# Two attentions on one core: copies of Q and K tied to their rounded parts, halo reads placed with Q, another order for the last output groups and for the first unit's value parts

## Chip, core and metric

The kernel runs on one core of one Trainium2 chip. The metric is the device time of one execution in microseconds (us). The core has five engines that the text names: TensorE (PE in the profile; PEld is its weight load), VectorE (DVE), ScalarE (ACT), GpSimd (POOL) and SyncE (SP). SyncE does no arithmetic here; it issues the DMAs that copy Q and K, and a DMA that waits on its queue holds up those behind it.

## What is computed

Two attention layers over separate inputs, each with S = 2048 positions, D = 1024 and 32 heads of 32. B attends to a sliding window of 256 positions; A attends to 8 positions at a distance of 2.

```python
def _A_ref(x, wqkv, wo):
    H = 32; Dh = D // H
    W, dil = 8, 2
    qkv = (lambda x, *d: x.transpose(*d))((x @ wqkv).reshape(B, S, 3, H, Dh), 2, 0, 3, 1, 4)
    q, k, v = qkv[0], qkv[1], qkv[2]
    ...
    logits = jnp.einsum("bhsd,bhswd->bhsw", q, kg) * scale
    logits = jnp.where(mask[None, None, :, :], logits, -1e9)
    attn = _softmax(logits, axis=-1)
    o = jnp.einsum("bhsw,bhswd->bhsd", attn, vg)
    return (lambda x, *d: x.transpose(*d))(o, 0, 2, 1, 3).reshape(B, S, D) @ wo

def _B_ref(x, wqkv, wo):
    H = 32; Dh = D // H; W = 256
    ...
    scores = jnp.einsum("bhqd,bhkd->bhqk", q, k) * (Dh ** -0.5)
    idx = jnp.arange(S)
    mask = (idx[:, None] - idx[None, :] >= 0) & (idx[:, None] - idx[None, :] < W)
    scores = jnp.where(mask[None, None], scores, -1e9)
    p = _softmax(scores, axis=-1)
    o = jnp.einsum("bhqk,bhkd->bhqd", p, v)
    return (lambda x, *d: x.transpose(*d))(o, 0, 2, 1, 3).reshape(B, S, D) @ wo
...
return jnp.concatenate([a, b], axis=-1)
```

## The kernel before

**Units, slots, head groups.** Each layer's 2048 positions are cut into four chunks of 512, so there are eight units: 0 to 3 are layer B (called dense: 256 positions back), 4 to 7 are layer A (called windowed; its even and odd positions are sorted apart, so that distance 2 becomes distance 1). A unit that continues the one before it has a halo: units 1, 2, 3, 5 and 7 read the last K columns of the unit before. In each unit the 32 heads are taken in eight slots of four heads. Unit u, slot s is head group 8u + s; there are 64.

**Two parts of every number.** Every operand of a projection is held as a rounded part and a low part (the difference to the rounded one), and a product is three matmuls (`TERMS`, L30). `Stream` (L87) loads each weight or input tile of 128 x 1024 into one of three raw buffers, by GpSimd's DMA queue after the first eight, and `parts` (L126) splits it: VectorE casts (L129), and VectorE (L137) or GpSimd (L134) subtracts. Weights go whole into one of three w tiles; inputs are split in halves into ten x tiles.

**The work of a slot.** `qk_items` (L298) multiplies for Q, then K: 24 wide matmuls each (L363). `evac` (L311) lets ScalarE write the rounded part out of PSUM (L314) and VectorE the low part (L318). Then `stack` (L323) issues three copies (L328) by SyncE into a stacked tile, `qst` or `kst`, of 96 rows: rounded, rounded, low for Q and rounded, low, rounded for K, so that one score matmul over 96 rows sums the three products. There are two `qst` and two `kst`, used in turn; `waiting` holds a stack back until the head group two before has given out its result. For units with a halo, `read_halo` (L304) issues three more reads into `kst`, and L333 writes the halo of the next unit. `attention` (L589) then makes a first pass of 16 scores (L614) whose row maximum (L619, VectorE) and exponential sum (L624, ScalarE) give the log sums; these go through a small transpose (L653) and by SyncE (L660) as two more rows into `qst`. A second pass (L696 dense, L509 windowed) has the logarithm of the sum already in it; ScalarE takes the exponential, masks follow on VectorE or GpSimd, and the matmuls with V (L741, L548) give the result `ot`, again in two parts (L577, L581). `v_items` (L395) makes the values of a unit in four parts, in the slots of `V_SLOTS`; `o_items` (L438) multiplies a finished unit by wo, in the slots of `O_SLOTS` of the next unit, eight groups of 24 wide matmuls (L455). A group's result is copied to the single staging tile `ost` (`NST` is 1; L379 ScalarE or L382 VectorE) and stored by ScalarE's queue (L470). For the last unit, `TAIL` groups run seven of their eight steps (a step is one head group's `ot`) before the last head group has its result, and the eighth step after it; the other groups follow whole.

**The order.** `tc.manual_schedule()` is on: every engine runs its instructions in the order in which the Python program emits them. That order comes from a planner, the loop at L803: it holds a clock of its own (`Clock`, L33) with a price for every operation, takes from four sequences (log sums, second passes, first passes, projections) the item that could start first, and emits it. `done["stack"]` tells when the planner believes K's copies to have landed, `done["nat"]` when a Q or K is copied out. The chip does not see this clock: there each instruction waits on semaphores for its operands.

## Time and profile before

| | |
|---|---|
| time, median of 3 runs | 1974.42 us (1971.13 to 1975.38) |
| time of the profiled execution | 1973.82 us |
| its span, first to last instruction | 1972.1 us |
| mean granted clock of TensorE | 0.987 |
| busy: TensorE, VectorE, ScalarE, GpSimd | 98%, 66%, 49%, 36% |

A share is of the span. A row of the timeline gives the start, how long the row's instructions take together, the engine, the line, what is written and read, and in brackets the idle time of the engine before it with what ended it. A row of the chain gives start, length and what was on the chain that ended last. A row of stretches gives the bounds, the length, the busy time of PE, PEld, DVE, ACT and POOL with their counts of instructions, the granted clock of TensorE, the share of the DMA engines and the GB/s. A row of waits names who waited for whom: us in total, times, longest.

### The profile page before, as it was taken

To read this page: it belongs to the slowest core of one execution; us is meant where nothing else is said; L and a number is where in the kernel's file an instruction comes from. 1 tells how busy PE (TensorE), PEld (TensorE's weight loads), DVE (VectorE), ACT (ScalarE), POOL (GpSimd) and SP (SyncE) were. 2 spreads that over 40 slices of the span, in tenths; PEclk is the share of its full clock that TensorE was granted. 3 is DMA by queue.
4 is the path that set the end of the run, shared out by engine and by line. 5 is a ranking of instruction groups with operands and counts; after the bars stand their busy time and mean duration, and the time that the engine had idled before them with its cause. 6 is when DMAs were issued, how large, how long until landed. Compare 5 with 4: busy or idle time off the path is not lost.

```text
span 1972.1 us, 36479 instructions
## 1 busy us (share of the span) xinstructions
PE 1924.7 (98%) x12608; PEld 1619.8 (82%) x12608; DVE 1295.7 (66%) x3762; ACT 957.5 (49%) x3137; POOL 708.7 (36%) x923
## 2 busy tenths in 40 slices
PE   7999999999999999999999999999999999999998
PEld 6878887888877878788878888978888788888886
DVE  5687776678665786567865657655666557666653
ACT  3565554475654656555563344423534334434441
POOL 4334343444433434443443323233332333233221
PEclk9999999999999999999999999999989999999998
DMA  5555546455546465345645647455553565556442
GB/s 176 150 139 153 160 124 178 132 153 157 152 136 174 121 189 149 117 140 148 177 119 146 173 139 196 128 149 170 149 163 116 174 177 162 141 146 172 136 126 75
DMA packets 136502, 294.92 MB, mean 150 GB/s; under 512 B 14464, under 2 KB 42112, under 8 KB 136320
## 3 DMA queue, kind: packets, MB, share of 16 engines
q1 hardware_dynamic: 85632, 124.82, 26.1%
q0 software_dynamic: 40320, 146.82, 22.9%
q10 hardware_dynamic: 10368, 20.98, 2.9%
q8 instruction: 100, 1.64, 0.4%
q14 instruction: 82, 0.67, 0.1%
HBM read 163.58 MB, written 27.26 MB: 97 GB/s over the span
## 4 chain that ended last, share of the span: by engine, by line
PE 84%; DVE 7%; DMA 6%; ACT 2%; issue 1%; SPq 0%; POOL 0%; DVEq 0%; ACTq 0%; POOLq 0%
PE g L363 31%; PE g L455 16%; PE g L415 16%; PE s L614 7%; PE s L696 5%; PE o L741 4%; PE s L509 3%; DMA qst<-rt 3%; PE o L548 2%; DMA kst<-nat 1%; DMA raw<-xs 1%; DVE x L137 1%; DVE w L129 1%; ACT s L624 1%; DVE w L137 1%
## 5 line engine op out<-in xcount | busy, mean ns | idle before, releaser
L363 PE MATMUL g<-x,w 128*128 128x512 f32 x3072 | 801.9, 401 | 8.6 <-DVE w L129 8.0
L134 POOL TENSOR_TENSOR w<-raw,w 128x512 fp32r<-128x512 f32 x225 | 392.5, 1745 | 897.2 <-PE s L614 285.7
L363 PEld LDWEIGHTS g<-x,w 128*128 128x128 f32 x3072 | 562.0, 191 | 110.9 <-DVE w L129 8.4
L624 ACT ACTIVATE s<-s,nm 128x384 f32<-128x384 f32 (+3 forms) x1024 | 452.3, 443 | 231.0 <-DVE nm L619 227.1
L415 PE MATMUL g<-w,x 128*128 128x256 f32 x3072 | 413.3, 285 | 0.0
L415 PEld LDWEIGHTS g<-w,x 128*128 128x128 f32 x3072 | 392.7, 191 | 1.9 <-issue 0.6
L455 PE MATMUL g<-ot,w 128*128 128x512 f32 x1536 | 384.2, 397 | 3.6 <-DVE w L129 2.9
L455 PEld LDWEIGHTS g<-ot,w 128*128 128x128 f32 x1536 | 283.8, 190 | 58.1 <-DVE w L129 3.6
L619 DVE CUSTOM_DVE_ANT_0 s<-s,mask_d 128x384 f32<-128x384 f32 (+2 forms) x512 | 262.0, 556 | 72.9 <-PE s L614 71.5
L614 PE MATMUL s<-kst,qst 96*128 96x384 f32 (+3 forms) x1024 | 238.7, 303 | 16.2 <-ACT s L624 7.1
L701 ACT ACTIVATE pbuf<-s 128x384 f32<-128x384 f32 (+2 forms) x480 | 197.1, 507 | 85.5 <-PE s L696 81.8
L614 PEld LDWEIGHTS s<-kst,qst 96*128 96x128 f32 x1024 | 181.3, 192 | 60.5 <-ACT s L624 18.1
L624 ACT ACTIVATION_READ_ACCUMULATOR s<-s,nm 128x1 f32 x1024 | 210.2, 205 | 0.0
L619 DVE CUSTOM_DVE_ANT_0 s<-s,mask_w 128x136 f32<-128x136 f32 (+1 forms) x512 | 142.4, 322 | 98.4 <-PE s L614 96.8
L129 DVE CAST w<-raw 128x1024 fp32r<-128x1024 f32 x256 | 199.9, 781 | 9.4 <-PE g L455 9.4
L137 DVE TENSOR_TENSOR w<-raw,w 128x512 fp32r<-128x512 f32 x287 | 197.2, 696 | 8.8
L682 POOL TENSOR_SCALAR_AFFINE_SELECT pbuf<-pbuf 128x128 f32<-128x128 f32 (+1 forms) x383 | 147.9, 404 | 150.1 <-ACT pbuf L701 143.5
L314 ACT ACTIVATE nat<-g 128x512 fp32r<-128x512 f32 x128 | 76.6, 598 | 255.2 <-PE g L363 247.8
L318 DVE SCALAR_TENSOR_TENSOR nat<-g,nat 128x512 fp32r<-128x512 f32 x128 | 88.3, 690 | 145.5 <-ACT nat L314 134.9
L524 DVE TENSOR_TENSOR pbuf<-pbuf,keep_w 128x272 f32<-128x272 f32 (+1 forms) x224 | 116.9, 566 | 61.5 <-ACT pbuf L514 60.6
L619 DVE DVE_READ_ACCUMULATOR2_ANT nm<- 128x1 f32 x1024 | 144.3, 141 | 0.0
L696 PEld LDWEIGHTS s<-qst,kst 98*128 98x128 f32 x704 | 106.2, 189 | 37.8 <-PE o L741 10.0
(48 smaller groups left out, 1227.3 us busy)
## 6 DMA issues: line engine op xcount, KB each, us to landing
raw<-wqk POOLq DMA_DIRECT2D x126, 512.0 KB, 3.7
qst<-nat SPq DMA_DIRECT2D x192, 256.0 KB
kst<-nat SPq DMA_DIRECT2D x192, 256.0 KB
raw<-wo POOLq DMA_DIRECT2D x64, 512.0 KB, 3.7
raw<-wv POOLq DMA_DIRECT2D x62, 512.0 KB, 4.5
outs<-ost ACTq DMA_DIRECT2D x64, 256.0 KB
raw<-xs POOLq DMA_DIRECT2D x28, 512.0 KB, 4.8
halo<-nat SPq DMA_DIRECT2D x40, 256.0 KB
```

Source lines behind the costliest of these rows:

```text
L129: nc.vector.tensor_copy(t[:, 0, :], raw)
L134: nc.gpsimd.tensor_tensor(o, a, b, op=ALU.subtract)
L137: nc.vector.tensor_tensor(o, a, b, op=ALU.subtract)
L363: nc.tensor.matmul(h["ps"], h["w"][:, a, k * P:(k + 1) * P], xt[u][k][:, b, :], start=(k == 0 and i == 0), stop=(k == NK - 1 and i == 2))
L415: nc.tensor.matmul(ps, xt[u][k][:, a, p0:p0 + P], h["w"][:, c, k % kw], start=(k == 0 and i == 0 and r == 0), stop=(k == NK - 1 and i == 2 ...
L455: nc.tensor.matmul(h["ps"], h["w"][:, a, k * P:(k + 1) * P], ot[u, k][:, b, :], start=(k == 0 and i == 0), stop=(k == NK - 1 and i == 2))
L614: nc.tensor.matmul(ps[:, :n], q[0:96, j, b * P:(b + 1) * P], kk[0:96, j, c0:c1], start=True, stop=True)
L619: nc.vector.tensor_tensor_reduce(ps[:, :n], ps[:, :n], mask[:, cut:full], scale=-1.0, scalar=BIG, op0=ALU.add, op1=ALU.min, accum_out=nm)
L624: nc.scalar.activation(ps[:, :n], ps[:, :n], AF.Exp, bias=nm, scale=-1.0, accum_out=sm)
L682: nc.gpsimd.affine_select(w, w, pattern=[[0, m], [step, n]], compare_op=ALU.is_ge, fill=0.0, base=base, channel_multiplier=chan)
L696: nc.tensor.matmul(ps[:, i * n:(i + 1) * n], kk[0:98, j, 256 + kb * P:256 + (kb + 1) * P], q[0:98, j, q0:q0 + n], start=True, stop=True)
L701: nc.scalar.activation(w, ps[:, :pack * n].rearrange("p (j n) -> p j n", j=pack), AF.Exp)
```

## The change

The copies out of the rounded part are put into the program when the rounded part is begun (`stack_hi`), the copy out of the low part when that is made (`stack`); both use `place`. The halo reads stand ahead of Q's copies, and no longer ahead of K's. The last unit's output groups have `TAIL` 4: four groups run seven eighths early; group 3 accumulates in a bank of the score ring `rs`, and the weights of groups 3 to 7 (kind "xw") are split in halves into x tiles. In the first unit the value parts stand in slots 0, 2, 4, 7. Two prices of the planner change: a load by GpSimd's queue and VectorE's score pass. Line numbers of the diff are those of the source before and after.

```diff
@@ -24,8 +24,9 @@
 VPARTS = ((0,2),(2,2),(4,2),(6,2))
 V_SLOTS = {0: 0, 1: 1, 5: 2, 7: 3}
 O_SLOTS = {2: (0, 1), 3: (2, 3), 4: (4, 5), 5: (6, 7)}
+V0_SLOTS = {0:0,2:1,4:2,7:3}
 NX, NST = 10, 1
-TAIL, LAND, XAT = 2, 0.45, 1
+TAIL, LAND, XAT = 4, 0.45, 1
 C1, C3, CG, CV = 0.114, 0.2, 0.231, 0.243
 TERMS = ((0, 0), (0, 1), (1, 0))
 
@@ -60,7 +61,7 @@
 
     def fetch(self, dur, *ready):
 
-        t = max(self.use("pool", 1.0, *ready) + 0.6, self.free["loads"])
+        t = max(self.use("pool", 0.6, *ready) + 0.9, self.free["loads"])
         self.free["loads"] = t + dur + 0.5 * max(0.0, min(2 * dur, self.free["copies"] - t))
         return self.free["loads"] + LAND
 
@@ -109,7 +110,7 @@
             i = self.split
             self.load_to(i + 1)
             raw, t0 = self.raw.pop(i)
-            if self.items[i][0] == "x":
+            if self.items[i][0] != "w":
                 self.tiles[i], self.ready[i] = [], []
                 for h in range(2):
                     t = self.xpool.tile([P, 2, S], F32R, tag="x", name="x")
@@ -120,7 +121,7 @@
                 self.ready[i] = self.parts(t, raw, t0)
                 self.tiles[i] = t
             self.split += 1
-            end = self.ready[i] if self.items[i][0] != "x" else max(self.ready[i])
+            end = self.ready[i] if self.items[i][0] == "w" else max(self.ready[i])
             self.ck.defer(end, lambda n=i + NRAW + 1: self.load_to(n))
 
     def parts(self, t, raw, t0):
@@ -173,8 +174,9 @@
             if u and s in O_SLOTS:
                 plan += [("o", u - 1, n) for n in O_SLOTS[s]]
             plan.append(("qk", u, s))
-            if s in V_SLOTS:
-                plan.append(("v", u, V_SLOTS[s]))
+            vs = V_SLOTS if u else V0_SLOTS
+            if s in vs:
+                plan.append(("v", u, vs[s]))
         if u + 1 < U:
             plan.append(("x", u + 1))
     plan += [("o", U - 1, n) for n in range(NG)]
@@ -195,7 +197,7 @@
     for p in plan:
         ly = units[p[1]][0]
         if p[0] == "o":
-            item(p, "w", wo[ly, p[2]])
+            item(p, "w" if p[1] < U - 1 or p[2] < 3 else "xw", wo[ly, p[2]])
         elif p[0] == "v":
             s0, n = VPARTS[p[2]]
             for g in range(n):
@@ -321,24 +323,37 @@
                 rg.give(bank, e)
 
                 def stack():
-                    if t == 1 and has_halo:
-                        read_halo()
-                    dst, c = (qst[buf], 0) if t == 0 else (kst[buf], 256)
-                    for i, a in enumerate((0, 0, 1) if t == 0 else (0, 1, 0)):
-                        nc.sync.dma_start(dst[i:96:3, :, c:c + S].bitcast(F32), hl[:, a, :].bitcast(F32))
-                        e2 = ck.copy(0.95, e, ck.now)
+                    e2 = place(1, e)
                     if t == 1:
-                        done["stack"][u, s] = e2
+                        done["stack"][u, s] = max(e2, h2["hi"])
                     if t == 1 and u + 1 < U and units[u + 1][3]:
                         nc.sync.dma_start(halo[u % 2][s], hl[:, :, 256:].bitcast(F32))
                         e2 = ck.copy(0.95, e, ck.now)
-                    done["nat"][hg, t] = e2
-
+                    done["nat"][hg, t] = max(e2, h2["hi"])
+
+                later(stack)
+
+            def place(part, e):
+                dst, c = (qst[buf], 0) if t == 0 else (kst[buf], 256)
+                for i, a in enumerate((0, 0, 1) if t == 0 else (0, 1, 0)):
+                    if a == part:
+                        nc.sync.dma_start(dst[i:96:3, :, c:c + S].bitcast(F32), hl[:, a, :].bitcast(F32))
+                        e2 = ck.copy(0.95, e, ck.now)
+                return e2
+
+            def stack_hi():
+                if t == 0 and has_halo:
+                    read_halo()
+                h2["hi"] = place(0, r)
+
+            def later(f):
                 if hg < 2 or hg - 2 in done["o"]:
-                    stack()
+                    f()
                 else:
-                    waiting.setdefault(hg - 2, []).append(stack)
-
+                    waiting.setdefault(hg - 2, []).append(f)
+
+            h2 = {}
+            later(stack_hi)
             ck.defer(r, low)
 
         for t in range(2):
@@ -438,24 +453,32 @@
     def o_items(u, n):
         h = {}
 
+        last = u == U - 1
+        ring = rs if last and n == 3 else rg
+
         def ready(k):
             if (u * NG + k) not in done["ot"]:
                 return None
             if k == 0:
                 st.split_to(where["o", u, n] + 1)
-                h["r"] = st.ready[where["o", u, n]]
-                return latest(rg.when(), h["r"], done["ot"][u * NG])
-            return done["ot"][u * NG + k]
+                r = st.ready[where["o", u, n]]
+                h["r"] = r if isinstance(r, list) else [r, r]
+                return latest(ring.when(), h["r"][0], done["ot"][u * NG])
+            return max(done["ot"][u * NG + k], h["r"][k // 4])
 
         def run(k):
             if k == 0:
-                h["ps"], h["b"] = rg.take()
-                h["w"], _ = st.get(where["o", u, n])
+                h["ps"], h["b"] = ring.take()
+                w, _ = st.get(where["o", u, n])
+                h["w"] = [(w[i // 4], i % 4 * P) if isinstance(w, list) else (w, i * P) for i in range(NK)]
+            w, c = h["w"][k]
             for i, (a, b) in enumerate(TERMS):
-                nc.tensor.matmul(h["ps"], h["w"][:, a, k * P:(k + 1) * P], ot[u, k][:, b, :],
+                nc.tensor.matmul(h["ps"], w[:, a, c:c + P], ot[u, k][:, b, :],
                                  start=(k == 0 and i == 0), stop=(k == NK - 1 and i == 2))
-            if k == 3 and (u < U - 1 or n != TAIL - 1):
-                st.split_to(where["o", u, n] + 2)
+            if k == 3 and (not last or n == 0 or n > 2):
+                st.split_to(where["o", u, n] + (3 if last and n == 0 else 2))
+            if k == 5 and last and n in (1, 2):
+                st.split_to(where["o", u, n] + 3)
 
         def after(k):
             if k == NK - 1:
@@ -463,7 +486,7 @@
                 for f in list(stores.values()):
                     f()
                 o = stp.tile([P, S], F32, tag="ost", name="ost")
-                e = copy_out(o, h["ps"], h["b"], rg)
+                e = copy_out(o, h["ps"], h["b"], ring)
 
                 def store():
                     if stores.pop((u, n), None):
@@ -618,7 +641,7 @@
             def top():
                 nc.vector.tensor_tensor_reduce(ps[:, :n], ps[:, :n], mask[:, cut:full], scale=-1.0, scalar=BIG,
                                                op0=ALU.add, op1=ALU.min, accum_out=nm)
-                e = ck.use("dve", (n + 80) / 960, ck.now)
+                e = ck.use("dve", (n + 110) / 960, ck.now)
 
                 def total():
                     nc.scalar.activation(ps[:, :n], ps[:, :n], AF.Exp, bias=nm, scale=-1.0, accum_out=sm)
```

## The prediction

> **What bounds the kernel now.** I read the page first: span, busy shares, clock, chain of waits.
>
> ```profile
> span 1972.1 us, 36479 instructions
> PE 1924.7 (98%) x12608; PEld 1619.8 (82%) x12608; DVE 1295.7 (66%) x3762; ACT 957.5 (49%) x3137; POOL 708.7 (36%) x923
> PE 84%; DVE 7%; DMA 6%; ACT 2%; issue 1%; SPq 0%; POOL 0%; DVEq 0%; ACTq 0%; POOLq 0%
> ```
>
> TensorE is busy for 98% of the span and carries 84% of the chain; the next engine has a third of its time free. The change adds no matmul and takes none away (both programs hold the same number of each kind), so it can only move time through the 47.4 us in which TensorE is idle (1972.1 - 1924.7) and through the clock at which it runs. I therefore listed next what ends the waits of TensorE, over the whole span.
>
> ```profile
> PE s L614 <- ACT s L624: 7.1, 8, 1.2
> PE s L509 <- DMA qst<-rt: 6.7, 10, 1.8
> PE s L614 <- DMA kst<-nat: 5.7, 5, 2.0
> ```
>
> Columns: us in total, times, longest. Score matmuls (L614) wait for the copy of K into its stacked tile five times, 5.7 us in all, once for 2.0. The last reading is of stretches: busy time of each engine, then the granted clock.
>
> ```profile
> 1542.40:1545.80 3.40, 2.06 (x10) 1.36 (x8) 0.00 (x0) 0.59 (x1) 0.58 (x1) 1.00 1.07 328
> 1545.80:1549.20 3.40, 3.14 (x18) 2.79 (x19) 2.05 (x12) 1.97 (x10) 0.00 (x0) 1.00 0.58 223
> 1453.70:1463.90 10.20, 10.20 (x36) 8.95 (x36) 5.84 (x19) 4.83 (x16) 1.92 (x2) 0.50 0.41 115
> 1917.90:1921.30 3.40, 2.04 (x13) 1.51 (x12) 0.14 (x1) 0.10 (x1) 0.00 (x0) 1.00 0.02 5
> 1921.30:1938.40 17.10, 13.54 (x73) 9.99 (x73) 10.39 (x17) 4.24 (x10) 3.11 (x4) 0.50 0.18 61
> ```
>
> In 1453.70 to 1463.90 and in 1921.30 to 1938.40 the granted clock is 0.50: a wait on TensorE can cost more than itself. The latter follows a stretch in which TensorE had 2.04 us of work in 3.40. The first two rows show that it is not certain: as little work at 1542.40, and the clock stayed at 1.00 behind it. At half clock 17.1 us give 8.5 us of work less.
>
> **The copies of Q and K.** Stated aim: the copies of the rounded part leave while the low part is made. Here is one K of the kernel before (unit 6, slot 2, windowed), from its last matmul to the first score matmul.
>
> ```profile
> 1536.81 1.52 PE L363 MATMUL g<-x,w 128*128 128x512 f32 x6
> 1538.17 6.28 PE L455 MATMUL g<-ot,w 128*128 128x512 f32 x27
> 1538.37 0.60 ACT L314 ACTIVATE nat<-g 128x512 fp32r<-128x512 f32 x1 [4.84 <-PE g L363]
> 1539.00 1.93 SPq L328 DMA_DIRECT2D kst<-nat  x3
> 1539.01 0.69 DVE L318 SCALAR_TENSOR_TENSOR nat<-g,nat 128x512 fp32r<-128x512 f32 x1 [3.42 <-ACT nat L314]
> 1546.06 0.63 PE L614 MATMUL s<-kst,qst 96*128 96x128 f32 x4 [1.60 <-DMA kst<-nat]
> ```
>
> ScalarE ends the rounded part at 1538.97; the first copy is issued at 1539.00, before VectorE has begun the low part at 1539.01. The queue waits for data, not for the place in the source text, and the source already put a rounded copy first. VectorE is done at 1539.70, and the three issues last until 1540.93 at 0.64 each, so the low copy is ready before its turn. The edit only swaps the second and third copy of K; for Q it swaps nothing. On the chip it is worth 0.
>
> What does move is the planner's own clock. It dates the copies from the rounded part (time r) instead of the low part (time e), and its constants then put the end of K's three copies 5.32 us behind K's last matmul, where they gave 6.09 (0.82 to r, 0.77 more to e, 1.20 to issue, 3 x 0.95 to move, 0.45 to land; now the third copy waits only for the two before it, and the 0.77 falls out). The order of TensorE is written out from that clock, so the first score matmuls are set earlier. I counted the matmuls between K's last and the first score of each of the 64 head groups, in both programs, at the pace of the rows: 0.23 us for 512 columns, 0.125 for 256, 0.11 to 0.18 for the small ones.
>
> ```profile
> 44.23 5.49 PE g L363 x24
> 148.17 3.79 PE g L415 x30
> ```
>
> The cover's median falls from 8.2 to 6.3 us, its minimum from 6.1 to 5.5, and groups with under 6.6 us go from 7 to 36. An example: in unit 5, slot 2, 36 wide matmuls (8.2 us) stood between; now 27 (6.2).
>
> What is needed? In the fence above 7.73 us (1538.33 to 1546.06), of which the last copy takes 5.65 from its issue. The opposite bound is unit 4, slot 2, where the score starts without a wait 6.11 us behind K's end (1078.86 to 1084.97):
>
> ```profile
> 1540.32 5.65 DMA kst<-nat
> 1073.71 5.15 PE L363 MATMUL g<-x,w 128*128 128x512 f32 x22
> 1084.97 0.64 PE L614 MATMUL s<-kst,qst 96*128 96x128 f32 x4
> ```
>
> Summing the shortfall over all 64 groups, by what one copy is taken to need: 6.1 us gives 0 before and 5.6 after; 6.6 gives 1.6 and 21.8; 7.0 gives 5.8 and 36.2. The trace's own 5.7 us, spread over few long waits, says that the typical need is below 7.0; 7.73 for all is excluded, since it would give 17 before. I take 6.6, between the bounds: **22 us after, 16 more than now**; ends 0 and +30. TensorE runs in order, so the projection matmuls that could fill such a wait stand queued behind the score; VectorE, ScalarE and the next loads are late with it, and nothing of the wait lies beside other work.
>
> Some of these waits will halve the clock, as the first unit's did (the longest K wait, 2.0 us, then 3.4 us at 0.50):
>
> ```profile
> 30.30:33.70 3.40, 1.39 (x12) 1.22 (x11) 0.19 (x1) 0.00 (x0) 0.00 (x0) 1.00 0.93 297
> 33.70:37.10 3.40, 3.40 (x18) 3.40 (x18) 3.13 (x15) 2.31 (x11) 1.75 (x2) 0.50 0.04 14
> ```
>
> With needs from 6.1 to 7.7 on covers near 5.9, some six of 36 would exceed 1.3 us. If half of them cost one stretch of 3.4 us at 0.50 (1.7 us), that is 5, less 1.7 that this first wait has already: **+3**, ends 0 and +12.
>
> **Halo reads.** They go with Q instead of K. Before, in unit 5, slot 2:
>
> ```profile
> 1301.87 1.86 SPq L328 DMA_DIRECT2D qst<-nat  x3
> 1303.78 2.05 SPq L308 DMA_DIRECT2D kst<-halo  x3
> 1306.69 0.60 ACT L314 ACTIVATE nat<-g 128x512 fp32r<-128x512 f32 x1 [4.84 <-PE g L363]
> 1307.31 1.95 SPq L328 DMA_DIRECT2D kst<-nat  x3
> ```
>
> The reads left 2.9 us before K's rounded part was even begun; K's copies are not behind them. Ahead of Q they can add at most their 2.05 us of issue to Q, whose score stands 11.3 us or more behind Q's last matmul in the new order: 0 either way. The row of log sums (qst<-rt) is never put behind a waiting halo read in the new queue order; once, in unit 0, it stands behind two Q copies.
>
> **The end.** Four output groups instead of two run seven eighths before the last window, group 3 in a score bank, and the weights of groups 3 to 7 are split in halves into x tiles (for VectorE two short casts in place of a long one, and both subtractions, while TensorE has 5.5 us of work a group). Before:
>
> ```profile
> 1917.51 0.22 PE L653 MATMUL s<-ident,hl 128*32 128x128 f32 x1
> 1918.07 0.67 SPq L660 DMA_DIRECT2D qst<-rt  x1
> 1920.52 3.80 PE L509 MATMUL s<-qst,kst 98*128 98x8 f32 x20 [1.36 <-DMA qst<-rt]
> 1926.45 0.59 ACT L577 CAST ot<-o 128x512 fp32r<-128x512 f32 x1 [1.50 <-PE o L548]
> 1927.09 3.23 PE L455 MATMUL g<-ot,w 128*128 128x512 f32 x6 [0.70 <-ACT ot L577]
> 1929.08 0.59 ACT L379 COPY ost<-g 128x512 f32<-128x512 f32 x1 [2.04 <-PE g L455]
> 1931.83 0.69 DVE L382 COPY ost<-g 128x512 f32<-128x512 f32 x1 [4.06 <-DMA outs<-ost]
> 1932.43 0.69 DVE L129 CAST w<-raw 128x1024 fp32r<-128x1024 f32 x1
> 1933.17 1.22 PE L455 MATMUL g<-ot,w 128*128 128x512 f32 x2 [2.85 <-DVE w L129]
> ```
>
> Three waits (1.36 + 0.70 + 2.85 = 4.9) and 8.5 of half clock: 13.4 us. In the new order 15 wide matmuls (3.45) stand between L653 and the first window matmul, which needs 2.8: no wait. Twelve plus the 24 of group 3 (at least 5 us) lie between the last window matmuls and the first that needs the last ot: no wait. But there is still one output staging tile. The copies of groups 1, 2 and 3 all stand on VectorE, each behind the landing of the store before it (copy ended 1929.67, next began 1931.83: 2.16, plus 0.60 for itself), and the split of group 5 stands behind them. From the start of the last eighths: ScalarE's copy ends at 1.45, the three copies begin at 3.6, 6.4 and 9.1, the cast at 9.7, the matmul at 10.2. TensorE has 4 x 0.69 + 5.5 = 8.3 us to do. So a wait of 1.9, and behind it likely 1.7 to 3.4 of half clock: some 4.4 instead of 13.4, **-9**; ends -12 (no wait, no half clock) and -3.
>
> **First unit, prices.** The value parts of unit 0 move from slots 1, 5, 7 to 2, 4, 7; its TensorE waits other than K's are under 1 us each. The prices (VectorE's score pass, POOL's loads) move 54 instructions from VectorE to POOL and elsewhere; both have the time (66% and 36%). Where a unit ends, in units 4 to 6, the row of log sums gets 5.5 us of cover instead of 3.3 to 4.7; in units 1 and 2, slot 6, it gets 2.1, under the 3.14 that this copy takes here:
>
> ```profile
> 1185.43 3.14 DMA qst<-rt
> ```
>
> Together **-1**, ends -8 and +6.
>
> **Sum** on the profiled execution (1973.8 us, 0.6 under the median shown): +16 + 3 - 9 - 1 = +9: 1982.8, and against the median **1983**.
>
> **A rule against the trace.** The row at 1917.90 had 1.36 us of idle in a 3.40 us stretch and was followed by half clock. The Trainium skill, "TensorE: Matmul & The Clock Gate", "What's actually happening", says that the clock falls back only after a whole idle window of about 3.4 us; by that no wait here would cost clock, and the trace disagrees (0.50 after 1.36 us of idle).
>
> **Rivals.**
> - Slower still: K needs 6.9 or more as a rule, and every second wait over 1 us halves the clock. +27 + 12 - 8 = 2005. For it: 7.73 above. Against: only five such waits before.
> - Faster: the scores' wait on K. If K's copies, with nothing beside them, need about 6.1, the waits stay at 5.7, the end gives 9 and the unit ends 3: 1962. It decides at a need of about 6.3, where the waits after reach 12 and the sum is 0. For it: the row at 1084.97. Against: the wait at 1546.06 behind 6.28 us of work.
> - No change: a wait on K makes up for a later wait on loads or log sums (7.1 and 6.7 us are there to be absorbed), so that 9 of the 16 vanish: 1974.
> - Waits cost only themselves: no half clock follows waits of under 3 us, at K or at the end. 1983 - 3 - 2.5 = 1978 (2.5 is the end's half clock). Against it: the two rows at 0.50. The rule of the Trainium skill above would give this case.
>
> **How the numbers follow.** Chances: forecast 0.48 (its own range 1977 to 1993), slower still 0.16, faster 0.20, no change 0.10, waits alone 0.06. About 0.2% is what a measurement of this kernel can tell: under 1970.5 is faster, over 1978.4 slower. The last case lies at the edge, and I count half of it as slower: faster 0.20, same 0.13, slower 0.67. The range takes half of each outer rival: 1963 to 2000.
>
> **What would show it.** Right: TensorE waits for kst<-nat some 25 to 36 times, near 22 us in all; K's first copy still issued within 0.1 us of ScalarE's end, the last at 2.0; one wait of about 2 us at group 5 of the end, and the span from the last log-sum row to the end shorter. Wrong: kst<-nat waits under 10 us, or K's copies landing sooner after K's last matmul than now, or a gain at unit ends over 8 us.

## The result, and the profile after

| | before | after |
|---|---|---|
| median of the runs compared | 1974.3 us | 2000.5 us (1991.8 to 2001.4) |
| ratio, 95% interval | | 1.0134 [1.0105, 1.0162] |
| time of the profiled execution | 1973.8 us | 1991.8 us |
| its span | 1972.1 us | 1990.0 us |

The kernel became 26 us slower; forecast were 9, with a range up to 2000. The profiled execution of after is its fastest; its granted clock is 0.994, that of the other three 0.990 to 0.991, so the traces show 18 of the 26 us. The page of after:

```profile
span 1990.0 us, 36510 instructions
PE 1924.5 (97%) x12608; PEld 1611.6 (81%) x12608; DVE 1277.4 (64%) x3708; ACT 955.2 (48%) x3130; POOL 744.8 (37%) x989
PE 80%; DMA 8%; DVE 6%; issue 2%; ACT 2%; POOL 1%; SPq 0%; DVEq 0%; ACTq 0%; POOLq 0%
```

TensorE is idle for 65.5 us (1990.0 - 1924.5) where it was for 47.4: 18.1 more, about the whole difference of the spans. Two further changes cancel. The clock was better (lost to it: 0.006 x 1990 = 12 us, before 0.013 x 1972 = 26). And TensorE's work at full clock, which is its busy time less what the clock took, grew by 13.5 us, from 1899.1 to 1912.6, for the same matmuls. Counted from start to start of the matmuls outside the half-clock stretches, 6 us of that lie in value matmuls of 384 columns; the rest is spread in pieces under 3.5 us. The profile models where a matmul ends, so a stall between two matmuls can stand in the busy time; what stalls here stays open. What ends the idle time, in the view of waits (us in total, times, longest):

```profile
PE s L637 <- DMA kst<-nat: 14.8, 15, 3.1
PE s L719 <- DMA qst<-rt: 6.9, 6, 1.7
PE s L637 <- issue: 5.5, 8, 2.3
PE s L532 <- DMA qst<-rt: 4.2, 8, 1.1
PE s L637 <- DMA kst<-halo: 2.9, 4, 1.0
PE g L476 <- DVE x L130: 2.1, 1, 2.1
```

L637 is the first pass of scores (L614 before). Its wait for K grew from 5.7 to 14.8 us, and some waits for K stand under other names: those put down to "issue" and to the halo read end at the same matmul. So below I count by place instead: the idle time straight before the first score matmul of each of the 64 head groups. That is **6.1 us (8 times) before, 24.4 (32 times) after**. The place that the prediction took as its example (unit 6, slot 2) in the timeline of after:

```profile
1560.68 0.84 PE L378 MATMUL g<-x,w 128*128 128x512 f32 x3
1561.36 6.28 PE L476 MATMUL g<-ot,w 128*128 128x512 f32 x27
1561.56 0.60 ACT L316 ACTIVATE nat<-g 128x512 fp32r<-128x512 f32 x1 [4.84 <-PE g L378]
1562.18 1.85 SPq L340 DMA_DIRECT2D kst<-nat  x3
1562.19 0.69 DVE L320 SCALAR_TENSOR_TENSOR nat<-g,nat 128x512 fp32r<-128x512 f32 x1 [3.42 <-ACT nat L316]
1569.98 0.63 PE L637 MATMUL s<-kst,qst 96*128 96x128 f32 x4 [2.35 <-issue]
```

The first copy leaves 0.02 us after ScalarE's end (1562.16), as before. At this place the same 27 matmuls of 6.28 us stand ahead of the score in both kernels. The score starts 8.46 us behind K's last matmul (1561.52), against 7.73 before: here the score was not put earlier, K came later, and the wait is 2.35 instead of 1.60. Over all 64 head groups the order did what the prediction counted: TensorE's work between K's last matmul and the first score has a median of 6.4 us, before 8.0, and 36 groups have less than 6.6, before 7.

The end of after, from the timeline, and then its stretches (busy time of the five engines, then the granted clock):

```profile
1932.22 0.92 PE L430 MATMUL g<-w,x 128*128 128x256 f32 x6
...
1942.37 0.22 PE L676 MATMUL s<-ident,hl 128*32 128x128 f32 x1 [0.57 <-DVE hl L668]
...
1960.02 0.59 ACT L394 COPY ost<-g 128x512 f32<-128x512 f32 x1 [5.77 <-PE g L476]
...
1962.78 0.69 DVE L397 COPY ost<-g 128x512 f32<-128x512 f32 x1 [7.81 <-DMA outs<-ost]
1965.64 0.69 DVE L397 COPY ost<-g 128x512 f32<-128x512 f32 x1 [2.17 <-DMA outs<-ost]
1968.51 0.69 DVE L397 COPY ost<-s 128x512 f32<-128x512 f32 x1 [2.18 <-DMA outs<-ost]
1969.12 0.42 DVE L130 CAST x<-raw 128x512 fp32r<-128x512 f32 x1
1969.59 6.69 PE L476 MATMUL g<-ot,x 128*128 128x512 f32 x27 [2.13 <-DVE x L130]
```

```profile
1965.49:1968.90 3.41, 1.97 (x9) 1.31 (x7) 1.08 (x2) 0.00 (x0) 0.00 (x0) 1.00 0.20 77
1968.90:1972.32 3.42, 2.73 (x11) 1.96 (x12) 3.32 (x8) 0.59 (x1) 0.00 (x0) 1.00 0.20 77
1972.32:1975.73 3.41, 3.41 (x17) 2.83 (x16) 3.15 (x7) 0.09 (x1) 0.00 (x0) 1.00 0.20 77
```

The chain of three copies, each behind the landing of the store before it, the split behind them and the one wait at group 5 came as forecast (2.13 us; forecast 1.9). The half clock behind it did not come here: 1.00 in all three stretches. From the last value matmul to the end, the kernel before took 65.2 us, from this row of its timeline to 1972.1; after takes 56.9 (1933.14 to 1990.0):

```profile
1906.01 0.93 PE L415 MATMUL g<-w,x 128*128 128x256 f32 x6
```

### The profile page after: what moved, and what is told of

It is laid out like the page before. It is cut to its first block, busy times and chain, and to the rows that moved or that the text cites. A ratio compares the mean times of both kernels' runs of the same rounds, so it can differ in the third digit from the quotient of the medians.

```text
span 1990.0 us, 36510 instructions
## 1 busy us (share of the span) xinstructions
PE 1924.5 (97%) x12608; PEld 1611.6 (81%) x12608; DVE 1277.4 (64%) x3708; ACT 955.2 (48%) x3130; POOL 744.8 (37%) x989
## 4 chain that ended last, share of the span: by engine, by line
PE 80%; DMA 8%; DVE 6%; issue 2%; ACT 2%; POOL 1%; SPq 0%; DVEq 0%; ACTq 0%; POOLq 0%
PE g L378 31%; PE g L476 15%; PE g L430 14%; PE s L637 7%; PE s L719 5%; PE o L764 4%; DMA kst<-nat 3%; PE s L532 3%; DMA qst<-rt 3%; PE o L571 2%; DVE x L138 1%; DMA raw<-xs 1%; DVE w L130 1%; DVE x L130 1%; ACT s L647 1%
## 5 line engine op out<-in xcount | busy, mean ns | idle before, releaser
L135 POOL TENSOR_TENSOR w<-raw,w 128x512 fp32r<-128x512 f32 x230 | 400.5, 1741 | 873.1 <-issue 255.2
L476 PE MATMUL g<-ot,w 128*128 128x512 f32 x1416 | 356.6, 395 | 0.0
L476 PEld LDWEIGHTS g<-ot,w 128*128 128x128 f32 x1416 | 258.7, 188 | 47.4 <-issue 0.8
L637 PE MATMUL s<-kst,qst 96*128 96x384 f32 (+3 forms) x1024 | 234.6, 304 | 31.4 <-DMA kst<-nat 14.8
L637 PEld LDWEIGHTS s<-kst,qst 96*128 96x128 f32 x1024 | 177.1, 191 | 78.3 <-issue 32.5
L705 POOL TENSOR_SCALAR_AFFINE_SELECT pbuf<-pbuf 128x128 f32<-128x128 f32 (+1 forms) x444 | 176.4, 417 | 149.0 <-ACT pbuf L724 144.2
L138 DVE TENSOR_TENSOR w<-raw,w 128x512 fp32r<-128x512 f32 x272 | 188.2, 698 | 8.7
L130 DVE CAST w<-raw 128x1024 fp32r<-128x1024 f32 x251 | 189.9, 757 | 2.4 <-DMA raw<-wv 2.4
```

Source lines behind the costliest of these rows:

```text
L130: nc.vector.tensor_copy(t[:, 0, :], raw)
L135: nc.gpsimd.tensor_tensor(o, a, b, op=ALU.subtract)
L138: nc.vector.tensor_tensor(o, a, b, op=ALU.subtract)
L476: nc.tensor.matmul(h["ps"], w[:, a, c:c + P], ot[u, k][:, b, :], start=(k == 0 and i == 0), stop=(k == NK - 1 and i == 2))
L637: nc.tensor.matmul(ps[:, :n], q[0:96, j, b * P:(b + 1) * P], kk[0:96, j, c0:c1], start=True, stop=True)
L705: nc.gpsimd.affine_select(w, w, pattern=[[0, m], [step, n]], compare_op=ALU.is_ge, fill=0.0, base=base, channel_multiplier=chan)
```

## The experiments

All are compared with the kernel before in the same sitting. "First scores" are the waits counted by place as above, "work" is TensorE's work at full clock; both are from the profiled execution, the work from the busy time and the mean clock of its page, to about 1 us.

| run | ratio to before, 95% interval | first scores, us (times) | work, us |
|---|---|---|---|
| before | 1 | 6.1 (8) | 1899 |
| after | 1.0134 [1.0105, 1.0162] | 24.4 (32) | 1913 |
| copies alone | 1.0140 [1.0109, 1.0171] | 25.0 (31) | 1911 |
| all but the copies | 1.0057 [1.0028, 1.0085] | 18.2 (15) | 1902 |
| old plan, new queue | 1.0048 [1.0025, 1.0070] | 6.8 (7) | 1898 |
| new plan, old queue | 1.0207 [1.0172, 1.0243] | 36.2 (36) | 1911 |
| new plan, halo reads alone early | 1.0127 [1.0102, 1.0151] | 24.2 (34) | 1913 |
| after, K's date put back | 1.0030 [1.0011, 1.0049] | 9.4 (9) | 1902 |
| after, prices put back | 1.0102 [1.0083, 1.0120] | 22.9 (31) | 1912 |
| after, date and prices put back | 1.0029 [1.0012, 1.0046] | 8.1 (10) | 1907 |
| prices alone | 1.0079 [1.0052, 1.0107] | 16.1 (14) | 1909 |
| end and prices | 1.0079 [1.0052, 1.0105] | 13.7 (11) | 1904 |
| POOL's price alone | 1.0059 [1.0039, 1.0080] | 7.7 (11) | 1903 |
| VectorE's price alone | 1.0099 [1.0072, 1.0125] | 17.2 (13) | 1904 |
| first unit alone | 1.0008 [0.9991, 1.0025] | 12.3 (14) | 1899 |
| K's date 0.4 us later on before | 1.0033 [1.0015, 1.0052] | 8.1 (10) | 1903 |
| semaphore price 0.18 for 0.17 | 1.0052 [1.0034, 1.0071] | 14.8 (10) | 1904 |
| semaphore price 0.16 for 0.17 | 1.0074 [1.0054, 1.0094] | 15.1 (13) | 1903 |

### The copies: the plan against the queue

The copies' part does two things: it changes what the planner believes (and so the order on all engines), and the order in which SyncE issues. Two kernels do the one without the other. Within each pair the orders of TensorE, VectorE, ScalarE and GpSimd are the same; only SyncE's differ. A call named `book` or `book_halo` enters a copy in the planner's clock without issuing it; `place` and `read_halo` issue in the place of the kernel after.

The copies' part alone, on the kernel before (the end, first unit and prices stay old):

> The kernel before with the copies and halo reads of the change, and nothing else of it (old end, old first unit, old prices). Plan theory (the planner dates K's copies 0.77 us earlier, the chip does not deliver them earlier): first-score waits rise from 6 to 20-26 us, time 1974 + 14 to 25 = 1988 to 1999. Queue theory (the new order in SyncE's queue holds up other transfers): the same time, but with the log-sum waits (second score, first matmul) up from 8 to over 14 as well. Rest theory (end, first unit and prices carry the loss): within 5 us of before.

All the rest of the change, without the copies' part:

> The changed kernel with copies and halo reads as before (new end, first unit and prices stay). Plan theory: first-score waits fall back to 6 to 10 us, the end keeps its gain; 1974 - 9 + up to 5 = 1963 to 1971. Queue theory: the same. Rest theory: stays at 1990 to 2001.

The old plan with the new queue:

```diff
 def stack():
+    place(1)
     if t == 1 and has_halo:
-        read_halo()
-    dst, c = (qst[buf], 0) if t == 0 else (kst[buf], 256)
-    for i, a in enumerate((0, 0, 1) if t == 0 else (0, 1, 0)):
-        nc.sync.dma_start(...)
+        book_halo()
+    for _ in range(3):
         e2 = ck.copy(0.95, e, ck.now)
...
+def stack_hi():
+    if t == 0 and has_halo:
+        read_halo()
+    place(0)
```

> The kernel before, with the copies and halo reads put into SyncE's queue as the change has them, while the planner still books them where and as it did: all other engines run the same order as before. Plan theory: 1972 to 1977, no change; K's three copies issued at 0.66, 1.26, 1.96 us behind K's last matmul instead of 0.66, 1.39, 2.01. Queue theory: slower by 5 to 20 us, with longer waits for qst<-rt and kst<-nat.

The new plan with the old queue:

```diff
 def stack():
-    e2 = place(1, e)
+    if t == 1 and has_halo:
+        read_halo()
+    for i, a in enumerate((0, 0, 1) if t == 0 else (0, 1, 0)):
+        nc.sync.dma_start(...)
+    e2 = book(1, e)
...
 def stack_hi():
     if t == 0 and has_halo:
-        read_halo()
-    h2["hi"] = place(0, r)
+        book_halo()
+    h2["hi"] = book(0, r)
```

> The mirror: the planner books the copies as the change does, SyncE's queue has them in the order of before. All other engines run the order of the kernel that has the copies alone. Plan theory: 14 to 25 us slower than before, within 3 us of the kernel with the copies alone. Queue theory: within 5 us of before.

Measured: 1.0140 for the copies alone, 1.0048 for the new queue alone, 1.0207 for the new plan alone. The plan is what costs: with it the first scores wait 24 to 36 us, without it 6 to 7. But the queue, which the prediction put at 0, is worth 15 us of gain under the new plan (2014.0 to 1998.9 us) and 12 us of loss under the old one (1970.3 to 1982.2). The gain shows in the waits of the kernel with new plan and old queue:

```profile
PE s L633 <- DMA kst<-nat: 22.0, 21, 3.6
PE s L633 <- DMA halo<-nat: 5.4, 3, 2.4
```

In the five units that read a halo the first scores wait 23.6 us there and 13.0 with the new queue; in the three others 12.6 and 12.0. That points at the halo reads, not at the swapped copies of K. A kernel that moves the reads alone tells the two apart:

```diff
 def stack():
-    if t == 1 and has_halo:
-        read_halo()
...
 def stack_hi():
     if t == 0 and has_halo:
+        read_halo()
         book_halo()
```

> The new plan of the copies in the old queue, with the halo reads alone moved to Q (order of TensorE, VectorE, ScalarE and POOL the same as in the two kernels with that plan). Old queue 1.0207 with 36 us at first scores, new queue 1.0140 with 24 us, of which 11 of the 12 us saved lie in the units that read a halo. Theory, that the halo reads move into K's time in the old queue and slow its copies: 1.013 to 1.016 and 23 to 27 us of first-score waits. Rival, that the swap of K's second and third copy saves: 1.019 or more, 33 us or more of waits.

Measured 1.0127, with 12.6 us at first scores in the units with a halo. Its row of waits:

```profile
PE s L632 <- DMA kst<-nat: 14.8, 15, 3.8
```

So the reads are the whole gain, and the swap of K's second and third copy is worth nothing that shows. For K's copies that were issued without delay in both kernels (26 head groups; the queue's packets counted off in the order of issue), the last packet landed 5.54, 5.89, 6.17, 5.99 and 5.90 us behind K's last matmul in units 1, 2, 3, 5 and 7 (means), against 6.00, 6.35, 6.42, 6.29 and 6.40 with the old queue: 0.2 to 0.5 us sooner. In units 0, 4 and 6, which read no halo, it was 0.1 later, the same, and 0.3 sooner. Where a score waited, it started 0.6 to 1.5 us behind that landing, mostly 0.9; with covers near 6.4 us a few tenths decide whether it waits. Why the same queue costs 12 us under the old plan was not settled: its second scores wait 14.2 us for the row of log sums in place of 9.1, and its clock is 0.984 in place of 0.987 (6 us); no run took these apart.

### K's date

The kernel after with the 0.77 us put back that fell out of the planner's date for K:

```diff
-                        done["stack"][u, s] = max(e2, h2["hi"])
+                        done["stack"][u, s] = max(e2, h2["hi"]) + 0.77
```

> The changed kernel with one number put back: the planner's date for K's stacked tile gets 0.77 us again, so that K's last matmul and the first score matmul are planned as far apart as before (counted in the order of TensorE: the median cover goes from 6.3 to 7.9 us, covers under 6.6 us from 36 to 11), while the copies keep their new order in the queue and the end, first unit and prices stay new. Theory, that the early date makes the score matmuls wait: waits at the first score matmuls of a head group fall from 24 us to 8 or less, and the time from 2000.5 to about 1984 (ratio 1.007). Rival, that the new order of the queue is what costs: the time stays at 1993 or more (1.012). Third possibility, that the new queue also lands K earlier here and costs nothing elsewhere: under 1976 (1.003).

Measured: 1977.9 us, 1.0030, 9.4 us at first scores. The date carries 1.0104 of the ratio (1.0134 / 1.0030), some 20 us; the rival, that the queue costs, is out for this order. The waits for K that are left:

```profile
PE s L637 <- DMA kst<-nat: 5.3, 3, 4.5
```

It was tried a second time, in the kernel after with both prices put back, with the early and with the put-back date:

> The changed kernel with both prices put back and K's early date kept. Against the run with date and prices back (1.0029) it differs by the date alone, in an order of its own. Theory, that the early date itself costs: first-score waits of 20 us or more (covers under 6.6 us: 40, against 13) and ratio 1.010 to 1.016, 15 to 25 us above that run. Rival, that the changed kernel as it stands is only an unlucky order: 1.004 or less.

> The changed kernel with K's date put back by 0.77 us and both prices put back: what is left of the change is the new order of the copies, the new end and the new first unit. If the date (20 us) and VectorE's price (15 us) are the two losses and add up, this run is 10 us or more below the run with the date alone put back (1977.9, ratio 1.003): 1965 to 1970, faster than before, with no log-sum matmul less than 2.5 us behind its last score. The rival, that the gains are given back elsewhere because the planner refills what is freed: ratio 1.000 to 1.004, as the run with the date alone.

```diff
-        t = max(self.use("pool", 0.6, *ready) + 0.9, self.free["loads"])
+        t = max(self.use("pool", 1.0, *ready) + 0.6, self.free["loads"])
...
-                e = ck.use("dve", (n + 110) / 960, ck.now)
+                e = ck.use("dve", (n + 80) / 960, ck.now)
```

1.0102 with the early date, 1.0029 without it: 14 us, and 22.9 against 8.1 us at first scores. Their rows of waits, the early date first:

```profile
PE s L637 <- DMA kst<-nat: 15.1, 15, 3.2
```

```profile
PE s L637 <- DMA kst<-nat: 5.3, 4, 3.6
```

So the early date costs 14 to 20 us in two surroundings. Not all of that is idle time: the five kernels with the early date have 1911 to 1913 us of work, the two with it put back 1902 and 1907. The expectation that date and prices add up, and that this last kernel beats the one before, failed: with the prices back it is as fast as with them (1976.5 and 1977.9 us).

### End, first unit, prices

> The kernel before with the two new prices alone (POOL's loads 0.6 + 0.9 instead of 1.0 + 0.6 in the planner, VectorE's score pass 110 instead of 80 columns dearer). The kernel with end, first unit and prices but without the copies had 13 us more than before, although its end was 6 us shorter; so 15 to 20 us must come from prices and first unit. Theory, that the prices move the row of log sums and the loads to worse places through all units: ratio 1.005 or more (1980 us or more), with more waits at the log-sum matmuls (9.7 us there against 5.5). Rival, that they are harmless, as I held in the prediction: within 1970 +- 4 us.

> The kernel before with the value parts of unit 0 moved to slots 2, 4, 7 alone. If the first unit carries the loss of the kernel without the copies: unit 0 itself gets longer and the ratio is 1.005 or more. In that kernel's profile unit 0 was only 1.3 us longer (196.9 against 195.6 us), which speaks against it: I expect 1970 +- 5 us (ratio 0.998 to 1.002), and a rest of the loss with the prices.

> The new end and the prices on the kernel before, without the copies and with the old first unit (the new end cannot be planned with the old prices alone). Theory: the price run's time less the end's gain of about 6 us (overhead from the last value matmul to the end 10 us or less, against 16.1). If the end's gain is real and adds up, this run stands 4 to 8 us under the run of the prices alone; the rival, that time won at the end is lost again elsewhere, has both within 2 us.

The three kernels take over those hunks of the diff word for word. The first unit is worth nothing that can be measured (1.0008; up to the first Q matmul of unit 1, unit 0 lasts 195.7 us, before 195.6). Its profiled execution does lose time just behind that: the first score of unit 0's last head group waits 2.9 us for K, before 0, and unit 1 lasts 265.4 us, before 259.2. The prices alone cost 15 us. With the end added, the median is the same (1988.6 and 1988.2 us, six runs each): the end's gain did not show in the time. In the trace it does. From the last value matmul to the end the eighteen profiled kernels fall into two groups: the twelve with the old end take 62.2 to 66.1 us (mean 64.0), the six with the new one 57.2 to 59.9 (mean 58.4; here counted from the start of that matmul). The new end is worth 5.6 us in the trace, about as much as the time of one such kernel is uncertain. In the kernel with end and prices the wait at group 5, here in a row of its timeline and then in two stretches, is followed by half clock:

```profile
1962.83 3.66 PE L463 MATMUL g<-ot,x 128*128 128x512 f32 x8 [2.12 <-DVE x L130]
```

```profile
1959.89:1963.30 3.41, 1.29 (x6) 0.65 (x4) 1.52 (x3) 0.00 (x0) 0.00 (x0) 1.00 0.21 77
1963.30:1966.72 3.42, 3.42 (x10) 2.52 (x9) 3.32 (x8) 0.59 (x1) 0.00 (x0) 0.50 0.40 151
```

The waits are 2.12 us here and 2.13 in the kernel after; one was followed by 0.50 and the other was not. The traces show a difference between them. In each of the eighteen, the half-clock stretches from 30 us on, but for one that the end cuts off, last whole multiples of 3.41 us and begin and end on one grid of that step, which lies differently in each execution. Here the whole wait lies in one step of the grid (1959.89 to 1963.30, 2.12 us idle). In the kernel after a bound of the grid, 1968.90, cuts the wait into 1.44 and 0.69 us. Between 30 and 1965 us the eighteen traces hold 47 single waits of TensorE of 1.7 to 2.6 us at full clock. The 25 that lie in one step were all followed by 0.50; of the 22 that a bound cuts, 6 were.

Then one price at a time:

> The kernel before with only the price of POOL's loads changed in the planner (0.6 + 0.9 instead of 1.0 + 0.6). The two prices together cost 15 us (ratio 1.0079). Counted in the order of TensorE, this one price alone moves little: covers of K as before (median 8.17 us, 7 under 6.6), covers of the log-sum row 4.77 us at the median against 4.80, none under 2.5. Theory, that VectorE's price does the harm: 1974 +- 5 us here (0.998 to 1.002). Rival, that loads issued at other times delay the weights: 1.005 or more.

> The kernel before with only VectorE's score pass priced 30 columns dearer in the planner. In the order of TensorE the log-sum matmul then stands less than 2.5 us behind the last score matmul in three head groups (before: in none), and the second scores less than 3.2 us behind the row in four (before: two). Theory, that this price alone does the harm, by moving the row of log sums and work from VectorE to POOL: ratio 1.006 to 1.010 (about 1988 us), 8 us or more of waits at the log-sum matmuls, 10 or more at first scores. Rival, that only both prices together do it: 1.003 or less.

1.0059 for POOL's alone, 1.0099 for VectorE's alone, 1.0079 for both. The theory that VectorE's price alone does the harm fell: the one that moves little in the order costs 0.6% as well, and the two do not add up. And the change opposite to the early date, on the kernel before:

```diff
-                        done["stack"][u, s] = e2
+                        done["stack"][u, s] = e2 + 0.4
```

> The kernel before with K's stacked tile dated 0.4 us later in the planner, and nothing else: covers of K from 8.2 to 9.6 us at the median, those under 6.6 us from 7 to 2. If waits for K are worth what the date's experiment says, the 6 us of first-score waits left before fall to 2 or less, and the time by 0 to 5 us (0.997 to 1.000). Rival: later scores press the rows and second scores of the same group (covers of these under 3.2 us go from 2 to 5), and the time rises by 4 or more (1.002).

1.0033, though covers of K are longer; the second scores wait 9.0 us for the row of log sums, before 9.1, which gives nothing to the rival either. Five of six small edits to the kernel before (the queue, both prices, each price alone, the date) had now cost 0.3% to 1.0%; the sixth, the first unit, had not. New theory: it is not the edits; the order of before is better than its neighbours.

### Another order, for no reason

One constant of the planner, the time of a semaphore, changed by 10 ns up or down:

```diff
-    SEM = 0.17
+    SEM = 0.18
```

> The kernel before with one constant of the planner (what a semaphore takes) at 0.18 instead of 0.17 us: 10 ns, without meaning for the chip, but the planner then writes another order of TensorE, about as different from that of before as the order of the kernel with the prices is. Theory, that the order of before is a lucky one among its neighbours: ratio 1.003 to 1.008, no single kind of wait to blame. Rival, that the prices (and K's date) do specific harm: 0.998 to 1.002.

```diff
-    SEM = 0.17
+    SEM = 0.16
```

> The same with 0.16 us instead of 0.17. Lucky order: 1.003 to 1.008 again. Specific harm: 0.998 to 1.002. If one of the two is slower and the other is not, the spread of orders is of this size, and no part that measures within 0.5% can be charged with it.

1.0052 and 1.0074: an edit that says nothing about the chip costs 10 and 15 us, as much as the prices. One thing that these orders have and that of before lacks shows at the ends of the dense units. The timeline of the kernel with 0.18, at the end of unit 3:

```profile
966.26 0.86 PE L363 MATMUL g<-x,w 128*128 128x512 f32 x3
...
983.97 2.18 SPq L308 DMA_DIRECT2D kst<-halo  x3
...
986.26 1.90 SPq L328 DMA_DIRECT2D kst<-nat  x3
...
997.91 0.59 PE L614 MATMUL s<-kst,qst 96*128 96x384 f32 x2 [3.91 <-DMA kst<-nat]
```

and of the kernel before:

```profile
965.75 0.86 PE L363 MATMUL g<-x,w 128*128 128x512 f32 x3
966.42 2.39 SPq L308 DMA_DIRECT2D kst<-halo  x3
969.23 1.92 SPq L328 DMA_DIRECT2D kst<-nat  x3
...
984.61 0.51 PE L614 MATMUL s<-kst,qst 96*128 96x384 f32 x2
```

The last K of the unit ends at the same time in both (967.12 and 966.61). Its stacked tile is free once slot 5 has given out its result: its last value matmuls end at 968.04 before, at 986.00 in the other order. So the copies leave 17 us later, behind the halo reads, and the score waits 3.9 us in place of none. At the last slot of units 0 to 3 first scores wait 0 us before, 7.8 with 0.18, 6.4 with 0.16, 5.7 with the prices alone and 3.6 in the kernel after. These waits are as much as 6 to 8 us of the 10 to 15 that the three orders lose. They are not the whole account: the first unit alone and the late date on before show 3.3 and 3.8 us there too and cost 0.1% and 0.3%, and the kernel with POOL's price alone has none of it. In the traces the three orders, POOL's price and the late date also have 3 to 10 us more work than before. How much of an order is changed does not tell what it costs: of 4928 score, log-sum and value matmuls, POOL's price moves 762 to another place among the projections, the two semaphore prices 2206 and 1780, and the first unit 411.

No kernel tried beats the one before.

## Why the prediction was wrong, point by point

**Direction and place: right.** TensorE as the bound, and K's early date as the cause, hold. Forecast were 22 us of waits at covers cut to 6.3 us, 16 more than now; by place the runs show 24.4, 18 more, and 14 to 20 us of time in two surroundings. The assumed need of 6.6 us fits too: K's copies that were issued at once landed 5.8 us behind K's last matmul (median of after), and waiting scores started 0.9 us behind that. The forecast of 25 to 36 waits holds by place (32); by the view's own name there are only 15, since the others carry the names "issue", halo read or log-sum row.

**"It can only move time" through idle time and clock: the step that failed.** The prediction's opening argument was that the change adds no matmul, so that nothing but TensorE's idle time and its clock can move. In the profiled execution of after, 18.1 us more are idle, 13.7 less are lost to the clock, and 13.5 us are neither: they are more work at full clock for the same matmuls. That goes with the order. With TensorE's order of before it is 1898 and 1899 us (the new queue does not touch that order), in the three kernels that share the new order of the copies alone 1911, 1911 and 1913, and in all other orders between 1899 and 1913. The other three executions of after had a clock of 0.990 to 0.991, some 7 us more lost; if their idle time and work were those of the profiled one, 18 idle, 13.5 work and 6 less lost to the clock make 26 (an estimate). The sum had no term for the work. What inside TensorE takes that time is not shown.

**The clock: +3 forecast.** The profiled execution of after lost 12 us to it against 26 before, the other runs 0.010 x 1998 = 20 us. More and longer waits did not cost more clock. The wait at 1969.59 and the equal one in the kernel with end and prices show, with the count of 25 and 22 waits there, that it matters where a wait lies on the grid of 3.41 us, which the prediction could not know; a term for it has a bound, hardly a value. The Trainium skill's rule in "TensorE: Matmul & The Clock Gate", "What's actually happening" (a whole idle window first), agrees with the row of after and disagrees with the row at 1963.30, where 0.50 followed an idle time of 2.12 us.

**The copies on the chip: worth 0, wrong in one half.** The swap is worth nothing, as forecast. "Halo reads: 0 either way" is not: 15 us of gain under the new plan, since K's copies land 0.2 to 0.5 us sooner in units with a halo, and a loss of 12 under the old plan. One of the prediction's own signs of being wrong, K landing sooner, thus came up: for copies issued at once the median landing is 5.8 us in after, 6.2 before. The step looked at when the reads are issued, and not at how long they hold up what follows them.

**The end: -9 forecast.** The chain of copies and its wait were right to 0.2 us. The trace gives 8.3 us against the kernel before and 5.6 as a mean over orders.

**First unit and prices: -1, the term that was mis-sized.** It was worked out from a few named covers that got longer or shorter. The first unit is indeed 0 (its TensorE waits "under 1 us each" leave out 8.0 us for the very first weights, the same in both kernels). The prices alone cost 15 us, all of the change but the copies 11 in spite of the gain at the end, and the 10 ns edits, which say nothing about the chip, 10 and 15: all above the range of -8 to +6. The order of TensorE was compared at the places that the change names, while part of the loss comes from places it does not name, such as the ends of units 0 to 3. What an order costs is no fixed price, though: in the kernel after, the prices are worth 6 us (1.0134 against 1.0102, intervals that overlap), and with K's date put back nothing (1.0030 and 1.0029).

**The sum by what was measured**, each step a ratio of kernels times 1972 us: all but the copies +11; from there to the kernel with K's date put back -5 (the new queue, in yet another order); the date +20; together +26. By another path: the copies alone +28, end and first unit -7, prices +6. The parts depend on the path, and added each on its own (28 and 11) they would give 39. On the second path the copies cost 9 us more than the forecast 19, with the waits as forecast, the prices 7 more than about -1, and the end came near its -9. Of the rivals, "slower still" gave 2005, nearest to the result, but by a long need of K and the clock; the need was as forecast and the clock did not get worse, so its number is luck.

## What to carry to other kernels

Where a planner writes the order, change one of its constants by a hair first and measure: that spread (here 0.5% to 0.7%, for a kernel that stands better than its neighbours) is what a new order alone can cost, and no part that measures within it can be charged with it. A planner's belief about a copy is an edit of its own: kernels that change the belief without the queue, and the queue without the belief, took two effects apart in one pair of runs. Compare the work at full clock as well as the idle time, since the same matmuls took 1899 us in one order and 1913 in another. Count waits by place in the order as well as by what the view names as the releaser, since one cause appeared here under four names.

## What was not expected of the hardware

With three halo reads issued between Q's and K's copies in place of ahead of Q's, K's last packet came 0.2 to 0.5 us later, although the reads were issued before K's rounded part was made. The clock went the other way than the idle time: 65.5 us idle with 0.994, 47.4 with 0.987. Equal waits of 2.1 us cost clock or not by where they lay on a grid of 3.41 us. And TensorE's work at full clock took 13.5 us longer for the same matmuls in another order, which no named wait explains.
